# Setting constants on VectorE, evacuating a transpose in chunks, and moving two gate tiles in a fused attention and MLP block

## The chip, the cores and the metric

The kernel runs on one core of one Trainium2 chip. The time is the device time of one execution in microseconds (us). The core has five engines with a queue each: TensorE (PE, matrix products), VectorE (DVE), ScalarE (ACT), GpSimd (POOL) and SyncE (SP, which here only issues DMAs). Products land in PSUM, which has eight banks of 128 partitions by 2 KB; DVE and ACT read them from there.

## The reference

For 2048 tokens of width 448, a layer norm without scale or shift gives `xn`. Two branches start from it.

```
qkv  = xn @ wqkv                      # 16 heads of 28
phi(t) = where(t > 0, t + 1, exp(t)) + 1e-6
kv   = sum over tokens of phi(k) v    # per head, 28 x 28
z    = sum over tokens of phi(k)
s    = (phi(q) kv / (phi(q) z + 1e-6)) @ wo

h    = max(xn @ w1 + b1, 0) ** 2      # 1792 wide
g    = silu(h @ w2 + b2)
out  = x + s * g
```

Inputs and output are bfloat16.

## The kernel before, in words

Tokens come in 16 tiles of 128 (number `si`) or four groups of 512 (number `g`). The width of 448 is three chunks of 128 and one of 64. `xn` is stored 512 wide per token tile: its last 64 columns are copied once more behind column 448 (`dup`, L707, for tiles 0 to 3, and L490 for the others), so that the transposed tile has the 64-row chunk in both halves of the partitions and two 64-row products can run beside each other.

The kernel does not write instructions in a fixed order. Each helper adds operations to a `Program` with an engine, what they read and write, and an estimated duration. `schedule` (L88) then makes a list schedule. PE and SP keep the order in which their operations were added. ACT, DVE and POOL take, of the operations that are ready soonest, the one that is due first, where "due" is worked out backwards from PE's order. An operation with a rank (while `pr.hot` is set, L1097 to L1119) may run only in its written order among the ranked ones of its engine. `emit` (L235) adds semaphore waits. PSUM banks are given out by the schedule too: a new buffer takes the bank that comes free first.

The parts that matter here:

- **Constants.** POOL writes `ident` (identity for transposes), `kvm` (128 x 1792), `hmask`, `zmask`, `ehd` and `zsb` with memsets (L363 to L395, L853), and cuts masks out of `hmask` (2), `zmask` (8) and `ehd` (4) with affine selects. DVE writes only `wz` (zeros for dummy products) and `onesr` (L371, L372).
- **Start.** PE runs 50 dummy products (`warm`, L1064, L1095). Meanwhile x tiles 0 and 1 arrive in a DMA each, tiles 2 and 3 in one. Each tile takes statistics on DVE (`ln_stats`, L461 and L463), a reciprocal root on ACT (`ln_rstd`, L470 and L474), a normalisation on DVE (`ln_norm`, L481), and the `dup`.
- **First transposes.** `x_transpose0` (L713) transposes two token tiles on PE, chunk by chunk (L724), and copies the result out of PSUM to `xT`. For tiles 0 and 1 ACT copies chunks 0, 2 and 3 (L744), DVE chunk 1 (L750). For tiles 2 and 3 DVE makes two copies of two chunks each. All later tiles are transposed by DMA (L495).
- **First hidden products.** `pe_part` (L567) computes the first seven 128-row pieces of h for group 0 in two halves of 256 tokens (L695): part 0 from token tiles 0 and 1, part 1 from tiles 2 and 3.
- **The main run.** `quads` (L1073) takes units in fours: `K` (k of one token tile), `Q` (128 columns of q of a group), `H` (128 rows of h of a group). For K and Q, `phi` (L592) runs exp on ACT and two operations on DVE (L599, L606). For H, ACT adds the bias and takes the maximum (L666), and DVE or ACT squares (L680, L681). `qx` (L647) computes the last 64 columns of q. POOL sums phi(k) over tiles (`zsum`, L626).
- **Gate tiles.** `gg` (L954) computes one token tile of h @ w2 with 14 products, from all 14 squared pieces of its group; DVE adds b2 (L981). Tiles 0 to 3 are done early, between the quads.

The order of PE around the moved part is, in L1142 to L1146, quad H1.8 to H1.11, `qx(0)`, gate tiles 0 and 1, quad Q0.2 H1.12 Q1.0 H1.13. After it come the layer norm of tiles 12 to 15 and the quads of group 2.

Of the kernel before, what the change touches and what calls it, by code (L numbers as in the profile page):

```python
# [7 lines left out]
AF = mybir.ActivationFunctionType  # L8

P = 128  # L10
S, D, F = 2048, 448, 1792
# [33 lines left out]
class Program:  # L45
# [14 lines left out]
    def add(self, eng, emit, reads=(), writes=(), dur=0.2, alts=(), nbytes=0):  # L60
        reads = [p for r in reads for p in self.aliases.get(r, (r,))]
        op = Op(eng, emit, reads, writes, dur, alts, nbytes)
        op.lead = self.lead
        if self.hot is not None:
            self.hot += 0.01
            op.prio = op.rank = self.hot
        for t in op.reads:
            w = self.writer.get(t)
            if w is not None:
                op.raw.add(w)  # L70
            self.readers.setdefault(t, []).append(op)
        for t in op.writes:
            w = self.writer.get(t)
            if w is not None and w is not op:
                op.deps.add(w)
            for r in self.readers.get(t, ()):
                if r is not op:
                    op.deps.add(r)
            self.writer[t] = op
            self.readers[t] = [r for r in self.readers.get(t, ()) if r is op]  # L80
        op.raw.discard(op)
        op.deps |= op.raw
        for d in op.deps:
            d.succ.append(op)
        self.ops.append(op)
        return op
# [208 lines left out]
def bass_recurrent_scan__linear_attn_block__dense_activation_squared_relu__prompt_kernel(  # L295
    nc, A_x, A_wqkv, A_wo, B_x, B_w1, B_b1, B_w2, B_b2, out
):
    with ExitStack() as es:
# [47 lines left out]
        def pool(fn, writes, reads=(), dur=0.3):  # L346
            add("pool", fn, reads, writes, dur)
# [15 lines left out]
        pool(lambda e, _: e.memset(ident[:, :], 0.0), ["ident"])  # L363
        select(ident[:, :], "ident", [[-1, P]], 0, 1, 1.0, ALU.not_equal)
        pool(lambda e, _: e.memset(eps5[:, :], 1e-5), ["eps5"], dur=0.1)
        add("pool", lambda e, _: e.memset(kvm[:, :, :], 0.0), [], ["kvm"], 1.0).prio = -50.0

        def vset(ap, val, name, again=False, dur=0.08):
            add("dve", lambda e, _: e.memset(ap, val), [name] if again else [], [name], dur)

        vset(wz[:, :], 0.0, "wz")  # L371
        vset(onesr[:, :], 1.0, "onesr")  # L372
        pool(lambda e, _: e.memset(eps6[:, :], 1e-6), ["eps6"], dur=0.1)

        def late_constants():
            hv = hmask[:, :].rearrange("p (b j) -> p b j", b=HC)
            pool(lambda e, _: e.memset(hv, 1.0), ["hmask"])
            select(hv, "hmask", [[-DH, HC], [0, DH]], 0, 1, 0.0)
            select(hv, "hmask", [[DH, HC], [0, DH]], DH - 1, -1, 0.0)
            pool(lambda e, _: e.memset(zmask[:, :, :], 1.0), ["zmask"])  # L380
            for view, pat, base in (
                (zmask[:, 0:3, :], [[P, 3], [-DH, 32]], 0),
                (zmask[:, 3, :], [[-DH, 32]], 384),
                (zmask[:, 4, :], [[-DH, 32]], 320),
            ):
                select(view, "zmask", pat, base, 1, 0.0)
                select(view, "zmask", [[-a, n] for a, n in pat], DH - 1 - base, -1, 0.0)
            select(zmask[:, 3, :], "zmask", [[0, 32]], 63, -1, 0.0)
            select(zmask[:, 4, :], "zmask", [[0, 32]], -64, 1, 0.0)
            pool(lambda e, _: e.memset(ones[:, :], 1.0), ["ones"], dur=0.1)  # L390
            pool(lambda e, _: e.memset(ehd[:, :], 0.0), ["ehd"], dur=0.5)
            ev = ehd[:, :].rearrange("p (h j) -> p h j", h=NH)
            for g in range(NG):
                select(ev, "ehd", [[-1, NH], [0, DH]], -32 * g, 1, 1.0, ALU.not_equal, dur=0.6)
# [83 lines left out]
        def ln_norm(si):  # L478
            add(
                "dve",  # L480
                lambda e, _: e.tensor_scalar(  # L481
                    out=xn[:, si, 0:D], in0=x_tok[:, si, :], scalar1=mv[:, si, 0:1],
                    scalar2=rstd[:, si : si + 1], op0=ALU.subtract, op1=ALU.mult,
                ),
                [("x", si), ("mv", si), ("rstd", si)], [("xn", si)], 0.36,
            )
# [80 lines left out]
        def pe_part(us, part, cs=(0, 1, 2)):  # L567
            def f(e, _):
                last = None
                for k in cs:  # L570
                    for u in us:
                        last = u[2](e, slice(0, 128), k, k == 0, False, part)
                return last

            need = {("xTp", 2 * part, k) for k in cs} | {w for u in us for w in u[1]}
            banks = [u[0] for u in us]
            add(
                "pe", f, sorted(need, key=str) + (banks if part or cs[0] else []), banks,
                len(us) * len(cs) * MM(256) + 0.01,
            )  # L580
# [123 lines left out]
            reads = xnames(g) if full else []  # L704
            return b, reads + w1names(fi // 4), mm, lambda: h_out(b, g, fi), 512

        def dup(lo, hi):  # L707
            add(
                "dve", lambda e, _: e.tensor_copy(xn[:, lo:hi, D:512], xn[:, lo:hi, 384:D]),
                [("xn", k) for k in range(lo, hi)], [("xnd", k) for k in range(lo, hi)], 0.12,  # L710
            )

        def x_transpose0(lo, between=None):  # L713
            bs = [Buf("T"), Buf("T"), None, Buf("T")] if lo == 0 else [Buf("T")] * 4
            bs[2] = bs[0]

            def piece(cs, tail):
                def f(e, _):
                    last = None
                    for c in cs:  # L720
                        v = ps(bs[c])[:, :].bitcast(bf)
                        for k in (0, 1):
                            o = (c * 2 + k) * P
                            last = e.transpose(v[:, o : o + P], xn[:, lo + k, c * P : (c + 1) * P], ident[:, :])  # L724
                    return last

                add(
                    "pe", f, [(("xnd" if tail else "xn"), lo + k) for k in (0, 1)] + ["ident"],
                    list(dict.fromkeys(bs[c] for c in cs)), len(cs) * 0.114,
                )  # L730

            if lo == 0:
                piece((0, 1, 2), False)
                piece((3,), True)
            else:
                piece((0, 1, 2, 3), True)
            src = lambda c0, c1: (
                ps(bs[c0])[:, :].bitcast(bf)[:, c0 * 256 : c1 * 256].rearrange("p (c k t) -> p c k t", c=c1 - c0, k=2)
            )
            dst = lambda c0, c1: xT[:, lo : lo + 2, c0:c1, :].rearrange("p k c t -> p c k t")  # L740

            def on_act(c):
                return add(
                    "act", lambda e, _: e.activation(out=dst(c, c + 1), in_=src(c, c + 1), func=AF.Copy),  # L744
                    [bs[c]], [("xTp", lo, c)], 0.39,
                )

            def on_dve(c0, c1):
                return add(
                    "dve", lambda e, _: e.tensor_copy(dst(c0, c1), src(c0, c1)), [bs[c0]],  # L750
                    [("xTp", lo, c) for c in range(c0, c1)], 0.1 + 0.16 * (c1 - c0),
                )

            if lo == 0:
                on_act(0)
                on_dve(1, 2)
                on_act(2)
                between()
                return on_act(3)
            on_dve(0, 2)  # L760
            return on_dve(2, 4)

        def bias_columns():
# [86 lines left out]

                add("dve", zops, [b, "zmask", "zsb0"], [("zsb", v)], 0.2)

        pool(lambda e, _: e.memset(zsb[:, :, :], 0.0), ["zsb0"], dur=0.15)  # L853

        def fold_wo(c):
            b = Buf("M")
# [207 lines left out]
        def warm(n, cost=0.1, after=()):  # L1064
            def f(e, _):
                last = None
                for _i in range(n):
                    last = e.matmul(ps(wb)[:, 0:P], wz[:, :], wz[:, :], start=True, stop=True)
                return last

            add("pe", f, ["wz", *after], [wb], n * cost)
# [20 lines left out]
                x_transpose(si, si + step)  # L1092
            pr.lead = 0.0

        warm(50, 0.092)  # L1095
        H0 = {fi: hh(0, fi, fi >= 7) for fi in range(NF)}
        pr.hot = -100.0  # L1097
        ln_stats(0)
# [4 lines left out]
        ln_rstd(1, 2)  # L1103
        bias_columns()
        ln_norm(1)
        dup(1, 2)
        ln_stats(2)
        x_transpose0(0, lambda: ln_rstd(2, 3))
        ln_stats(3)
        ln_rstd(3, 4)  # L1110
        ln_norm(2)
        ln_norm(3)
        dup(2, 4)
        warm(6, 0.056)
        for c in range(3):
            pe_part([H0[i] for i in range(4)], 0, (c,))
# [1 line left out]
        t23 = x_transpose0(2)  # L1118
        pr.hot = None  # L1119
        pe_part([H0[6]], 0)  # L1120
        pe_part([H0[i] for i in range(4)], 1, (0, 1))
        pe_part([H0[i] for i in range(4)], 1, (2,))
        tails = lambda *u: pe_tails(*u, need=[("xTp", lo, 3) for lo in (0, 2)])
        tails(H0[0], H0[2])
        tails(H0[1], H0[3])
# [14 lines left out]
        for i in range(1, 8):  # L1140
            zsum(i)
        quads("H1.8 H1.9 H1.10 H1.11")  # L1142
        qx(0)
        gg(0)
        gg(1)
        quads("Q0.2 H1.12 Q1.0 H1.13")  # L1146
        ln(12, 16, lead=2)
        quads("K2.0 H2.0 K2.1 H2.2 K2.2 H2.1 K2.3 H2.3 H2.4 H2.5 H2.6 H2.7")
        for i in range(8, 12):
# [83 lines left out]
```

## Time and profile before

| | |
|---|---|
| median of 11 runs | 150.06 us (149.68 to 150.81) |
| the profiled execution's own time | 150.03 us |
| its span, first to last instruction | 148.3 us |
| mean granted TensorE clock | 0.998 |
| PE busy | 142.1 us (96%) |
| DVE busy | 97.5 us (66%) |
| ACT busy | 79.9 us (54%) |
| POOL busy | 36.8 us (25%) |

The 1.73 us between the span and the execution's time lie before its first and after its last recorded instruction. Times below are us from the start of the span. A busy time is the sum over the engine's instructions without overlap. DMAs and waits are not counted as busy. An instruction's row starts when it was sent to its engine, so an instruction that waits for the one before it or for a shared resource has a longer row. The page's cut of the span into 40 slices shows PE at nine tenths or more in all but the first three and the last. The chain that ended last is PE for 79% and DVE for 15%.

### The profile page before, as it was taken

How to read it: one execution, taken by the hardware profiler on the slowest of the kernel's cores; microseconds unless marked ns; L12 is line 12 of the kernel's file. 1: busy time of each engine (PE TensorE's matmuls, PEld its weight loads, DVE VectorE, ACT ScalarE, POOL GpSimd, SP SyncE). 2: the span in 40 equal slices, each digit the busy share in tenths (PEclk: the TensorE clock that was granted, in tenths of full speed). 3: DMA queues.
4: the chain of work that ended last, by engine and by line, in shares of the span. 5: the costliest groups of instructions: out<-in, count | busy, mean ns of one | idle time of the engine just before them, and what ended most of it. 6: DMA issues, size and time to landing. Idle time of an engine off the chain costs nothing.

```text
span 148.3 us, 2855 instructions
## 1 busy us (share of the span) xinstructions
PE 142.1 (96%) x1136; PEld 70.9 (48%) x1136; DVE 97.5 (66%) x215; ACT 79.9 (54%) x152; POOL 36.8 (25%) x55
## 2 busy tenths in 40 slices
PE   7889999999999999999999999999999999999990
PEld 7765444443444445444443554454444544545450
DVE  2879899999987896158999510069683517226343
ACT  3435897898886983188879721997411110310200
POOL 8850025253000353000650000000000908209100
PEclk9999999999999999999999999999999999999999
DMA  4998699910747000000000000000000111202112
GB/s 81 339 313 219 175 213 377 261 50 0 53 93 133 8 4 0 0 0 4 0 2 0 4 0 0 0 4 2 0 0 4 62 62 47 77 0 66 62 62 62
DMA packets 16025, 10.53 MB, mean 71 GB/s; under 512 B 7372, under 2 KB 15628, under 8 KB 16012
## 3 DMA queue, kind: packets, MB, share of 16 engines
q1 hardware_dynamic: 15824, 10.28, 26.4%
q8 instruction: 9, 0.15, 0.4%
q10 hardware_dynamic: 188, 0.07, 0.2%
q14 instruction: 4, 0.03, 0.1%
HBM read 6.94 MB, written 1.84 MB: 59 GB/s over the span
## 4 chain that ended last, share of the span: by engine, by line
PE 79%; DVE 15%; DMA 2%; ACT 1%; issue 0%; SPq 0%; DVEq 0%
PE pb L964 29%; PE pb L699 18%; PE pb L779 6%; PE pb L1018 6%; PE pb L616 5%; PE pb L640 5%; DVE r L680 3%; DVE xn L481 3%; DVE pk L606 2%; DMA x_tok<-in_A_x_dram 2%; PE pb L695 2%; DVE pk L599 1%; PE pb L1054 1%; DVE st L461 1%; PE pb L785 1%; PE pb L865 1%
## 5 line engine op out<-in xcount | busy, mean ns | idle before, releaser
L964 PE MATMUL pb<-w,r 128*128 128x448 bf16 x224 | 44.3, 353 | 0.6 <-DVE r L680 0.6
L666 ACT ACTIVATE r<-pb,b1f 128x512 bf16<-128x512 f32 x54 | 33.8, 690 | 10.0 <-PE pb L699 9.9
L699 PE MATMUL pb<-xT,w 64*128 64x512 bf16 (+1 forms) x291 | 38.5, 376 | 0.0
L964 PEld LDWEIGHTS pb<-w,r 128*128 128x128 bf16 x224 | 21.1, 98 | 21.8 <-issue 1.7
L626 POOL TENSOR_TENSOR zacc<-zacc,pk 128x448 f32<-128x448 f32 x13 | 14.4, 1106 | 40.7 <-DVE pk L606 40.2
L991 ACT ACTIVATE gbuf<-gbuf 128x448 bf16<-128x448 bf16 x15 | 8.5, 581 | 29.7 <-DVE gbuf L981 29.7
L1007 POOL TENSOR_TENSOR obuf<-obuf,x_tok 128x448 bf16<-128x448 bf16 x12 | 12.0, 1029 | 48.7 <-DVE obuf L1001 48.7
L699 PEld LDWEIGHTS pb<-xT,w 64*128 64x128 bf16 (+1 forms) x291 | 14.2, 94 | 16.6 <-issue 0.4
L981 DVE TENSOR_TENSOR gbuf<-pb,b2b 128x448 bf16<-128x448 f32 x15 | 9.3, 623 | 16.5 <-PE pb L964 16.4
L680 DVE TENSOR_TENSOR r<-r 128x512 bf16<-128x512 bf16 x34 | 18.0, 562 | 3.0 <-ACT r L666 3.0
L1001 DVE TENSOR_TENSOR obuf<-pb,gbuf 128x448 bf16<-128x448 f32 (+2 forms) x17 | 9.2, 592 | 7.2 <-PE pb L1018 4.7
L681 ACT ACTIVATE r<-r 128x512 bf16<-128x512 bf16 x22 | 13.3, 635 | 0.0
L616 PE MATMUL pb<-w_qkv,xT 64*128 64x448 bf16 x112 | 13.2, 349 | 0.0
L948 DVE TENSOR_TENSOR pqT<-pqT,pb 128x512 bf16<-128x512 bf16 x12 | 7.4, 681 | 8.6 <-PE pb L925 8.6
L461 DVE BATCH_NORM_STATS2 st<-x_tok 128x6 f32<-128x448 bf16 x16 | 9.3, 616 | 2.7 <-DMA x_tok<-in_A_x_dram 2.7
L640 PE MATMUL pb<-xT,w_qkv 64*128 64x512 bf16 x84 | 11.0, 376 | 0.0
L699 PE MATMUL pb<-xT,w_1r 64*128 64x512 bf16 x56 | 10.3, 377 | 0.0
L606 DVE SCALAR_TENSOR_TENSOR pk<-pb,pk 128x448 bf16<-128x448 f32 x16 | 9.7, 621 | 0.3
L594 ACT ACTIVATE pk<-pb 128x448 bf16<-128x448 f32 x16 | 7.8, 541 | 3.4 <-PE pb L616 3.4
L779 PE MATMUL pb<-pk,xn 128*128 128x448 bf16 x48 | 9.4, 353 | 0.0
L606 DVE SCALAR_TENSOR_TENSOR pqT<-pb,pqT 128x512 bf16<-128x512 f32 x12 | 8.3, 692 | 0.4
L616 PEld LDWEIGHTS pb<-w_qkv,xT 64*128 64x128 bf16 x112 | 5.5, 94 | 6.0
(89 smaller groups left out, 130.4 us busy)
## 6 DMA issues: line engine op xcount, KB each, us to landing
out_dram<-obuf SPq DMA_DIRECT2D x15, 112.0 KB, 1.7
w<-in_B_w_dram SPq DMA_DIRECT2D x1, 1568.0 KB, 9.3
x_tok<-in_A_x_dram SPq DMA_DIRECT2D x3, 448.0 KB, 4.4
w<-in_B_w_dram SPq DMA_DIRECT2D x3, 384.0 KB, 5.0
w_qkv<-in_A_wqkv_dram SPq DMA_DIRECT2D x3, 336.0 KB, 5.1
w_o<-in_A_wo_dram SPq DMA_DIRECT2D x1, 392.0 KB, 9.2
w_qkv<-in_A_wqkv_dram SPq DMA_DIRECT2D x6, 56.0 KB, 4.6
x_tok<-in_A_x_dram SPq DMA_DIRECT2D x2, 112.0 KB, 2.5
```

The costliest lines, as they stand in the source:

```text
L461: op = add("dve", lambda e, _: e.bn_stats(st6[:, si, :], x_tok[:, si, :]), [("x", si)], [("st", si)], 0.58)
L606: lambda e, _: e.scalar_tensor_tensor(out=slot, in0=ps(buf)[:, 0:n], scalar=1.0 + 1e-6, in1=slot, op0=ALU.add, op1=ALU.max),
L616: return e.matmul(ps(b)[:, 0:D], xT[rw, si, c, :], w_qkv[rw, c, D : 2 * D], start=start, stop=stop)
L626: lambda e, _: e.tensor_tensor(out=o[:, :], in0=pk[:, 0, :] if i == 1 else zacc[:, :], in1=pk[:, i, :], op=ALU.add),
L640: return e.matmul(ps(b)[:, 0:512], w_qkv[rw, c, m * P : (m + 1) * P], xT[rw, 4 * g : 4 * g + 4, c, :], start=start, stop=stop,)
L666: rl = lambda e, _: e.activation(out=slot, in_=ps(b)[:, 0:512], func=AF.Relu, bias=b1f[:, fi : fi + 1])
L680: return e.tensor_tensor(out=slot, in0=slot, in1=slot, op=ALU.mult)
L681: return e.activation(out=slot, in_=slot, func=AF.Square)
L699: return e.matmul(ps(b)[:, 0:512], lhs, xT[rw, 4 * g : 4 * g + 4, c, :], start=start, stop=stop, skip_group_check=not full,)
L779: last = e.matmul(ps(b)[:, 0:D], xn[:, si, c * P : (c + 1) * P], pk[:, si, :], start=(si == 0), stop=(si == NT - 1),)
L964: last = e.matmul(ps(b)[:, 0:D], r2[:, fi, si * P : (si + 1) * P], w_2[:, fi, :], start=(fi == 0 and part is None), stop=(fi == NF - 1),)
L1007: lambda e, _: e.tensor_tensor(out=ob, in0=ob, in1=x_tok[:, si, lo:hi], op=ALU.add),
```

## The change

Five memsets move from POOL to DVE, or to the beginning of DVE's program: `zsb`, `hmask`, `zmask`, `ehd` and `kvm`. The selects stay on POOL. The dummies are 43 instead of 50, with another estimate of their cost. The `dup` of tile 1 runs on ACT. That of tiles 2 and 3 becomes two, the first ahead of tile 3's normalisation. The evacuation of the second transposes is three copies (chunk 0, chunk 1, chunks 2 and 3) instead of two, and the products that read it are added chunk by chunk. `qx(0)` and gate tiles 0 and 1 come behind the quad Q0.2 H1.12 Q1.0 H1.13.

```diff
-        add("pool", lambda e, _: e.memset(kvm[:, :, :], 0.0), [], ["kvm"], 1.0).prio = -50.0
...
         vset(wz[:, :], 0.0, "wz")
         vset(onesr[:, :], 1.0, "onesr")
+        vset(zsb[:, :, :], 0.0, "zsb0")
+        vset(hmask[:, :], 1.0, "hmask", dur=0.15)
+        vset(zmask[:, :, :], 1.0, "zmask", dur=0.2)
+        vset(ehd[:, :], 0.0, "ehd", dur=0.3)
+        vset(kvm[:, :, :], 0.0, "kvm", dur=1.0)
...
-            pool(lambda e, _: e.memset(hv, 1.0), ["hmask"])
...
-            pool(lambda e, _: e.memset(zmask[:, :, :], 1.0), ["zmask"])
...
-            pool(lambda e, _: e.memset(ehd[:, :], 0.0), ["ehd"], dur=0.5)
...
-        def dup(lo, hi):
+        def dup(lo, hi, act=False):
+            if act:
+                add(
+                    "act",
+                    lambda e, _: e.activation(out=xn[:, lo:hi, D:512], in_=xn[:, lo:hi, 384:D], func=AF.Copy),
+                    [("xn", k) for k in range(lo, hi)], [("xnd", k) for k in range(lo, hi)], 0.2,
+                )
+                return
...
-            on_dve(0, 2)
+            on_dve(0, 1)
+            on_dve(1, 2)
             return on_dve(2, 4)
...
-        pool(lambda e, _: e.memset(zsb[:, :, :], 0.0), ["zsb0"], dur=0.15)
...
-        warm(50, 0.092)
+        warm(43, 0.106)
...
         ln_norm(1)
-        dup(1, 2)
+        dup(1, 2, True)
...
         ln_norm(2)
+        dup(2, 3)
         ln_norm(3)
-        dup(2, 4)
+        dup(3, 4)
...
-        pe_part([H0[i] for i in range(4)], 1, (0, 1))
-        pe_part([H0[i] for i in range(4)], 1, (2,))
+        for c in range(3):
+            pe_part([H0[i] for i in range(4)], 1, (c,))
...
         quads("H1.8 H1.9 H1.10 H1.11")
+        quads("Q0.2 H1.12 Q1.0 H1.13")
         qx(0)
         gg(0)
         gg(1)
-        quads("Q0.2 H1.12 Q1.0 H1.13")
```

## The prediction

> **What bounds the kernel.** I read the page first: TensorE (PE) is busy 142.1 of the 148.3 us span, VectorE (DVE) only 97.5. Nearly all of PE's work is fixed, so the question is where PE stands still. The list of PE's waits (us in total, times, longest us) gives all of it:
>
> ```profile
> PE pb L1068 <- DVE wz L369: 1.1, 1, 1.1
> PE pb L964 <- DVE r L680: 0.6, 1, 0.6
> PE pb L724 <- DVE xn L481: 0.5, 1, 0.5
> PE pb L724 <- DVE xn L709: 0.4, 1, 0.4
> PE pb L695 <- DVE xT L750: 0.2, 1, 0.2
> ```
>
> The first is the lead-in to the dummies and stays. Three belong to the first transposes, one (0.6) to gate tile 0. The chain that ended last (start, us, what) says which count:
>
> ```profile
> 1.26 2.98 DMA x_tok<-in_A_x_dram
> ...
> 9.47 0.26 DVE xn L709
> 9.73 0.05 issue
> 9.78 0.63 PE pb L724 x8
> 10.41 0.02 issue
> 10.44 0.44 DVE xT L750
> 10.87 0.05 issue
> 10.92 1.48 PE pb L695 x12
> ...
> 35.26 2.02 DVE r L680 x6
> 37.28 0.05 issue
> 37.33 5.47 PE pb L964 x28
> ```
>
> From 4.24, when the second x tile lands, until 10.92 the chain runs over DVE and ScalarE (ACT); then PE until 20.26, DVE until 37.28, PE to the end. So two points set the time: when PE starts at 10.92, and when the squares (L680) let gate tile 0 start at 37.33. The third view is the timeline up to 10.5 (start, us, engine, line, operation), first DVE's, then POOL's:
>
> ```profile
> 0.96 0.17 DVE L369 MEMSET onesr<- 1x128 bf16 x1
> 2.94 0.63 DVE L461 BATCH_NORM_STATS2 st<-x_tok 128x6 f32<-128x448 bf16 x1 [1.81 <-DMA x_tok<-in_A_x_dram]
> ...
> 5.42 0.49 DVE L709 COPY xn<-xn 128x64 bf16<-128x64 bf16 x1
> ...
> 6.13 0.59 DVE L709 COPY xn<-xn 128x64 bf16<-128x64 bf16 x1
> ...
> 8.97 0.47 DVE L481 TENSOR_SCALAR xn<-x_tok,mv,rstd 128x448 bf16<-128x448 bf16 x1 [0.32 <-ACT rstd L474]
> 9.47 0.25 DVE L709 COPY xn<-xn 128x128 bf16<-128x128 bf16 x1
> ```
> ```profile
> 5.41 0.47 POOL L391 MEMSET ehd<- 128x448 bf16 x1
> 6.02 3.16 POOL L357 TENSOR_SCALAR_AFFINE_SELECT ehd<-ehd 128x448 bf16<-128x448 bf16 x4
> ```
>
> The 64-column copies take 0.49 and 0.59, though the same copy of 128 columns (L490) takes 0.19 later, when POOL is idle. Each ends within 0.05 us of a POOL instruction: the ehd memset (5.88), and the first ehd select (6.02 + 0.67 = 6.69).
>
> **The memsets.** DVE gets zsb, hmask, zmask, ehd and kvm. From wz to onesr, 64 words took 0.07 us, one word a cycle of about 1 ns; wz is written as uint32, so the zero tiles cost half their columns: 80 + 224 + 896, and 112 + 160 fp32 words, 1472 words or 1.53 us. DVE's gap before the first statistics is 1.81 (1.13 to 2.94): they fit with some 0.2 to spare, and another 0.48 of idle time stands before the second statistics at 4.26, which alone are on the chain. Cost nothing; cover gone beyond some 0.7. [...] I take 1.53, since the wz row shows the packed form.
>
> **POOL.** It loses kvm (1.59), zmask, zsb, ehd and hmask memsets (0.24 + 0.23 + 0.47 + 0.19). ident comes first, the zmask selects start near 1.25 instead of 3.05. From the first zmask select to the first ehd select is now 2.97; without the zsb and ehd memsets and the gaps behind them (about 0.6) it is 2.35, so the ehd selects, 0.81 apart, start near 3.6, 4.4, 5.2, 6.0 and end near 6.8. They are not gone from the normalisation: they now stand under both norms and the first dup. [...] By the uncontended row (a copy at 0.19 or less) dup(0) loses its 0.3 and norm(1) is held by its rstd (5.66) until 6.0. [...]
>
> **dup of tile 1 to ACT.** It takes 0.20 to 0.25 there (L474's one column 0.20, L744's 256 columns 0.36), hidden under the six transposes before the tail that needs it (0.5). In ACT's queue it stands before L744's copies, which wait for those same transposes. On DVE 0.59 goes: the statistics of tile 2 run from 6.35 rather than 6.72. What is late next is ACT: its two L744 copies start near 6.95 instead of 6.70, rstd(2) (0.5) and the third copy (0.35) follow, so rstd(3) ends near 8.9, as now (8.93). So DVE's gain is caught there. Behind it norm(3) is free of POOL (0.33 rather than 0.47), dup(2) runs in DVE's 0.32 idle before norm(3), and dup(3) alone takes at most 0.19, likely 0.15, against 0.25. Second transposes near 9.49 instead of 9.78: **-0.29**. POOL's hmask selects are over by 7.6. PE's earlier block (18 products, 0.107 each, from about 7.4) ends by 9.4.
>
> **Chunk-wise evacuation.** The first product needs only chunk 0. A one-chunk copy took 0.26 (7.36), a two-chunk copy 0.44: **-0.17**. The second chunk lands 0.26 later, while four products (0.43) of the first run: one more instruction, hidden. H0[6] on PE fills the time meanwhile and ends about when the copy does. PE starts at 10.46, **-0.46** with both.
>
> **Fewer dummies.** The windows of the dummies (PE columns are busy us and count, edge-crossers counted twice):
>
> ```profile
> 3.50:4.00 0.50, 0.50 (x7) 0.50 (x6) 0.00 (x0) 1.00 0.65 211
> 4.00:4.50 0.50, 0.50 (x9) 0.50 (x7) 0.00 (x0) 1.00 1.01 319
> 4.50:5.00 0.50, 0.50 (x13) 0.50 (x11) 0.00 (x0) 1.00 0.99 329
> ```
>
> The rate doubles near 4.3. Seven fewer at 0.056 end 0.39 earlier, at 5.2, into idle time: nothing gained, nothing paid, if the fast rate stays.
>
> **The gate tiles moved.** Quad Q0.2 H1.12 Q1.0 H1.13 (3.03 us in the chain from 42.80) goes before qx(0), gate tiles 0 and 1. PE's own sum is the same; its data (weights, xT of tokens 0 to 7) are used earlier already. Its four PSUM banks are those of H1.4 to H1.7, which ACT has emptied by 34.4, before PE needs them at 35.1. Gate 0 on PE's path: 37.33 - 0.61 - 0.46 + 3.03 = 39.29. DVE must finish group 0's squares: 37.28, plus two phis moved ahead of them (2 x (0.28 + 0.69) = 1.94), less the part of the early start that DVE passes on. It is busy 16.70 of 17.00 us from 20 to 37, its statistics of tokens 8 to 11 wait for x until 16.93, so at most 0.3 passes: 38.9 to 39.2. PE and DVE meet; bounds for the wait left are 0 and 0.6 (all of it back), I take 0.1, near the balance. **-0.51.** K2 follows gate 1 at the same offset; its DMA transposes were issued at 37.41 and the first pair lands 3.7 later, against 44.7. They may be issued up to 2 us later without cost, and none of SP's loads stands behind them in need.
>
> **Sum.** -0.46 - 0.51 = -0.97. Span 148.3 to 147.33; the profiled run's own 150.03 has 1.73 around the span: 149.06; that run lies 0.03 under the median of 150.06. I say **149.1**.
>
> **Rivals.** (1) *No collision at the start*: POOL's selects fall between DVE's copies, norm(1) ends at 6.0, the chain gains another 0.35: 148.7. For it, the selects leave 0.14 gaps; against it, norms longer than these. (2) *DVE remains the bound at gate 0*: the moved phis, or norms beside POOL's sums (four took 2.82 at 32.44, 1.32 at 14.50), hold the squares; half to all the gain goes back: 149.55 to 150.05. (3) *PE goes back to half rate.* After 5.2 PE has one tiny transpose until 6.4, 1.2 idle rather than 0.46, then short bursts. [...] If it comes back for as long as the dummies needed to lift it (3.2 us from 1.05), the products of 7.4 to 10.6 cost half of that, 1.6: 150.7. [...]
>
> **How the numbers follow.** Forecast 0.52 (its own range 148.8 to 149.5), (1) 0.10, (2) 0.22, (3) 0.16. A measurement of this kernel tells about 0.2% (0.3 us) from no change. Forecast, (1) and half of (2) are faster: 0.73; the other half of (2) 0.11; (3) 0.16. The range 148.55 to 150.3 leaves out (3) and the tail of (1).
>
> **What would show it.** DVE's memsets end before 2.9; ehd selects lie at 3.6 to 6.8 and dup(0) still takes about 0.6; second transposes near 9.5, PE's unbroken run from about 10.5; the wait of L964 for L680 at 0.2 or less. Wrong if PE's matmul rate halves after 5.2, if gate 0 still waits 0.5 or more, or if a PSUM wait turns up at the moved quad.

## The result, and the profile after

The changed kernel takes 148.87 us (median of 13 runs, 148.75 to 149.8) against 150.07 for the kernel before. The ratio is 0.993, with a 95% interval of 0.9913 to 0.9946. The forecast was 149.1. In a second comparison on the chip the same kernel took 149.37 against 150.15 (0.9941, 0.9923 to 0.996). The experiments show the most likely reason why the two medians differ by half a microsecond.

The profiled execution took 148.77 us with a span of 147.0, 1.3 less than before. PE's waits, in the same form as before (us in total, times, longest us), are now these two:

```profile
PE pb L1076 <- DVE wz L368: 1.1, 1, 1.1
PE pb L732 <- DVE xn L482: 1.0, 1, 1.0
```

The lead-in to the dummies is as it was. The second wait is the end of the dummies until the first transposes, longer than before (0.5) because the dummies end earlier. The waits for the dup, for the evacuation and at gate tile 0 are all gone. The chain that ended last (start, us, what) shows the two points that the prediction named:

```profile
5.29 0.68 DVE xn L717
5.97 0.29 DVE xn L482
6.26 0.05 issue
6.31 0.62 PE pb L732 x8
6.93 0.34 PE pb L1076 x6
7.26 0.03 issue
7.29 2.14 PE pb L696 x18
9.43 0.52 PE pb L732 x8
9.95 0.02 issue
9.98 0.30 DVE xT L758
10.28 0.05 issue
10.33 1.48 PE pb L696 x12
...
38.05 1.10 PE pb L656 x8
39.15 5.40 PE pb L972 x28
```

PE's unbroken run starts at 10.33 instead of 10.92, 0.59 earlier. Gate tile 0 (L972) follows the product before it with no gap. Before, the chain came to it over VectorE, with a wait of 0.61. The two make 1.20 of the difference.

Between the first and the second transposes the chain now runs over PE alone: six more dummies and the 18 products on tiles 0 and 1, which end at 9.43. VectorE has its last dup done before that, at 9.26. In the kernel before it was VectorE's last dup (9.47 to 9.73) that let the second transposes start.

The timeline of VectorE, and behind it one row of POOL's, shows the start and the squares:

```profile
2.53 0.17 DVE L368 MEMSET onesr<- 1x128 bf16 x1
3.00 0.63 DVE L462 BATCH_NORM_STATS2 st<-x_tok 128x6 f32<-128x448 bf16 x1 [0.30 <-DMA x_tok<-in_A_x_dram]
...
4.49 0.77 DVE L482 TENSOR_SCALAR xn<-x_tok,mv,rstd 128x448 bf16<-128x448 bf16 x1
...
5.29 0.68 DVE L717 COPY xn<-xn 128x64 bf16<-128x64 bf16 x1
...
34.81 2.43 DVE L681 TENSOR_TENSOR r<-r 128x512 bf16<-128x512 bf16 x7
37.15 2.20 DVE L462 BATCH_NORM_STATS2 st<-x_tok 128x6 f32<-128x448 bf16 x4
39.27 0.28 DVE L600 TENSOR_SCALAR pqT<-pqT 128x512 bf16<-128x512 bf16 x1
```
```profile
3.64 3.13 POOL L357 TENSOR_SCALAR_AFFINE_SELECT ehd<-ehd 128x448 bf16<-128x448 bf16 x4
```

The memsets end at 2.70 and VectorE still waits 0.30 for x. The ehd selects run from 3.64 to 6.77, and under them the first normalisation takes 0.77 (0.36 before) and the first dup 0.68 (0.49). The last squares of group 0 end at 37.2, almost 2 us ahead of gate tile 0.

### The profile page after: what moved, and what is told of

Read it like the earlier page. It is cut to its first block, busy times and chain, and to the rows that moved or that the text cites. A ratio compares the mean times of both kernels' runs of the same rounds, so it can differ in the third digit from the quotient of the medians.

```text
span 147.0 us, 2842 instructions
## 1 busy us (share of the span) xinstructions
PE 141.5 (96%) x1129; PEld 70.6 (48%) x1129; DVE 96.6 (66%) x221; ACT 79.9 (54%) x153; POOL 34.2 (23%) x50
## 4 chain that ended last, share of the span: by engine, by line
PE 93%; DVE 3%; DMA 1%; issue 0%; DVEq 0%
PE pb L972 29%; PE pb L700 26%; PE pb L617 7%; PE pb L788 6%; PE pb L641 6%; PE pb L1026 6%; PE pb L696 3%; PE pb L1062 2%; PE pb L656 1%; DMA x_tok<-in_A_x_dram 1%; PE pb L794 1%; PE pb L873 1%; DVE st L462 1%; PE pb L732 1%; DVE xn L482 1%; PE pb L933 1%
## 5 line engine op out<-in xcount | busy, mean ns | idle before, releaser
L972 PE MATMUL pb<-w,r 128*128 128x448 bf16 x224 | 44.3, 353 | 0.0
L972 PEld LDWEIGHTS pb<-w,r 128*128 128x128 bf16 x224 | 21.1, 98 | 21.1 <-issue 2.4
L681 DVE TENSOR_TENSOR r<-r 128x512 bf16<-128x512 bf16 x34 | 16.2, 508 | 3.9 <-ACT r L667 3.9
```

What stands on the lines that cost most here:

```text
L681: return e.tensor_tensor(out=slot, in0=slot, in1=slot, op=ALU.mult)
L972: last = e.matmul(ps(b)[:, 0:D], r2[:, fi, si * P : (si + 1) * P], w_2[:, fi, :], start=(fi == 0 and part is None), stop=(fi == NF - 1),)
```

## The experiments

There were twelve runs, in three groups. Each is set against the kernel before on the same chip (150.23, 150.15 and 150.10 in the three groups). Line numbers are those of each kernel's own file, so the same line can stand some lines further down than in the kernel before.

### The gate tiles alone

```diff
         quads("H1.8 H1.9 H1.10 H1.11")
+        quads("Q0.2 H1.12 Q1.0 H1.13")
         qx(0)
         gg(0)
         gg(1)
-        quads("Q0.2 H1.12 Q1.0 H1.13")
```

> The kernel before with the quad Q0.2 H1.12 Q1.0 H1.13 moved ahead of qx(0) and gate tiles 0 and 1, nothing else. Theory (two separate bounds, the start of PE's unbroken run and gate tile 0): the run still starts near 10.9, the wait of gate tile 0 for L680 (0.6) is gone, so the time is 0.5 to 0.6 us lower. Rival (VectorE holds gate tile 0 also at its later place): a wait of 0.3 or more comes back at gate tile 0 or at the moved quad, and the gain is 0.3 or less.

It took 149.52, a ratio of 0.9961 (0.9945 to 0.9978), or 0.6 less (0.71 between the two medians). In its profile the run starts at 10.80, as it would before, and gate tile 0 waits for nothing. PE's waits do have one line that the first profile of the kernel before did not have:

```profile
PE pb L699 <- ACT r L666: 0.3, 1, 0.3
```

This line does not come from the move. The load of x tiles 4 to 7 landed late in this execution, at 12.40, and the second profile of the kernel before has the same line (more on this load below). So the move is worth its 0.6 alone. The rival is out: PE's waits have no line for gate tile 0, which starts at 39.98, behind the products of `qx(0)` (L655), which PE began at 38.88.

### The first 11 us alone

The reverse of the diff above, applied to the changed kernel.

> The changed kernel with gate tiles 0 and 1 back at their old place, so only the edits of the first 11 us. Theory: PE's unbroken run starts 0.5 to 0.6 earlier (near 10.35), but VectorE, full from 20 to 37 us, passes on only part of it; gate tile 0 waits 0.8 to 0.9 instead of 0.6, and the time is 0.3 to 0.4 lower. Rival (the two gains simply add): gate tile 0 waits 0.6 as before, and the time is 0.6 lower. Together with the gate move alone, the theory's two runs add up to less than the 1.2 of the whole change, the rival's to all of it.

It took 150.36, a ratio of 1.0009 (0.9994 to 1.0025): no gain at all. Both expectations missed. The profile, of one of its fastest executions (149.53), makes it stranger: the run starts at 10.39 and gate tile 0 waits 0.62, so there the start passes on 0.5. Most executions lost it somewhere that this profile does not show.

### The selects taken out of the way

```diff
-            for g in range(NG):
-                select(ev, "ehd", [[-1, NH], [0, DH]], -32 * g, 1, 1.0, ALU.not_equal, dur=0.6)
+        def ehd_selects():
+            ev = ehd[:, :].rearrange("p (h j) -> p h j", h=NH)
+            for g in range(NG):
+                pool(
+                    lambda e, _, g=g: e.affine_select(
+                        out=ev, in_=ev, pattern=[[-1, NH], [0, DH]], compare_op=ALU.not_equal, fill=1.0,
+                        base=-32 * g, channel_multiplier=1,
+                    ),
+                    ["ehd"], ["ehd", ("xnd", 3)], dur=0.6,
+                )
...
         pr.hot = None
+        ehd_selects()
```

> The changed kernel with the four ehd selects on POOL made to wait for the dup of token tile 3, so that they run behind the first transposes; the hmask selects come ahead of them, near 3.6. Theory (the selects shut VectorE's normalisations and copies out): the rows of the first normalisation and the first dup fall from 0.77 and 0.68 to about 0.36 and 0.2, the first transposes start 0.3 to 0.8 earlier than 6.31, and PE's unbroken run starts 0.3 to 0.7 earlier than 10.33, with the time as much lower. Rival (these rows are long for another reason, or ACT or the arrival of w1 or x bounds the start instead): rows unchanged, or rows short and PE's run at 10.2 to 10.4, the time within 0.1 of the changed kernel's.

It took 149.53 (148.5 to 150.23), where the changed kernel had 148.87 and 149.37 in other groups. Here is VectorE's timeline of the first normalisation and dup:

```profile
4.54 0.36 DVE L491 TENSOR_SCALAR xn<-x_tok,mv,rstd 128x448 bf16<-128x448 bf16 x1
4.94 0.18 DVE L726 COPY xn<-xn 128x64 bf16<-128x64 bf16 x1
```

The collision is gone. The rows fall to 0.36 and 0.18, the first transposes start at 5.88 and the run at 10.00. As to the rows the theory holds. The time, expected to be 0.3 to 0.7 lower, did not fall: PE waits 1.1 later on, and the chain that ended last, between 9 and 18 us, says for what:

```profile
6.57 5.90 DMA x_tok<-in_A_x_dram
12.48 0.02 issue
12.50 2.21 DVE st L471 x4
14.70 0.29 DVE mv L473 x4
14.99 0.02 issue
15.02 0.31 ACT vep L480
15.32 0.02 issue
15.35 0.20 ACT rstd L484
15.55 0.59 ACT r L676
16.14 0.05 issue
16.18 1.04 PE pb L709 x8
```

The load of x tiles 4 to 7, issued near 6.6, lands at 12.48. VectorE's statistics of these tiles wait for it, ACT's reciprocal roots wait for the statistics, and behind the roots in ACT's queue stand the operations (L676) that empty PSUM banks. PE gets no bank until 16.18. An earlier start runs into this all the same, so in such an execution it is worth nothing.

### The same two kernels once more

> The kernel before, unchanged, for a second profile of its first 11 us. In the first profile the statistics of token tile 1 wait for its x until 4.26, in that of the changed kernel they run at 3.76 already. [...] Rival (the change itself made the x tiles land earlier): it lands at 4.2 to 4.3 again, and every profile of a kernel with the changed start shows 3.8 or less.

The second profile of the kernel before (150.21) has the statistics of tile 1 at 3.72, not 4.26, and the second transposes at 9.50, so the first profile showed a late x tile 1. And it has this row of VectorE:

```profile
12.28 2.21 DVE L461 BATCH_NORM_STATS2 st<-x_tok 128x6 f32<-128x448 bf16 x4 [1.36 <-DMA x_tok<-in_A_x_dram]
```

In the first profile these statistics started at 11.41. The load was issued at 6.59 in both. PE's run starts 0.28 earlier than in the first profile (10.64), yet gate tile 0 starts 0.17 later (37.50), behind squares that end at 37.45. That is how the run with the first 11 us alone can have lost its gain: with x late, VectorE's chain to the squares follows x, not PE.

> The changed kernel, unchanged, beside the three that follow. The x tiles 4 to 7 landed at 10.7 in its first profile, and at 11.3 to 12.5 in those of the other kernels, which issue the same loads in the same order. Theory (this landing differs between executions, and where it is late VectorE's statistics of tiles 4 to 7, and on ACT the reciprocal roots that wait for them, hold back the first emptying of PSUM banks, so that PE waits at L700 near 15): executions spread from 148.75 to 149.9, with single values near 148.75 where x lands before about 11. Rival (the changed kernel itself makes x land early): executions stay within 0.1 of 148.75.

The changed kernel spread from 148.78 to 150.02 over 12 executions, four of them at or below 148.84. Over both groups it has 25 executions with a median of 149.16, 0.9 to 1.0 below the kernel before. The second profile (148.84) starts its run at 10.32 and the statistics of tiles 4 to 7 at 11.59, and PE does not wait: a landing up to there is covered. None of its slower executions was caught in a profile, so that they have a late landing is concluded from the next run.

### The load of x tiles 4 to 7 moved ahead of wk

```diff
-        load_k("sp", w_qkv, A_wqkv, "wk", D, 2 * D)
         load_x(4, 8)
+        load_k("sp", w_qkv, A_wqkv, "wk", D, 2 * D)
```

> The changed kernel with the load of x tiles 4 to 7 issued ahead of the three loads of wk instead of behind them, nothing else (1.8 us earlier on SP's queue). Theory (the late landing of x 4 to 7 is what spreads the times and costs the slower executions up to 1 us): VectorE waits for no x at the statistics of tile 4, PE does not wait for ACT at L700, and the median is 148.6 to 148.8, with most executions inside 0.2. Rival (the spread comes from elsewhere, or wk then lands too late for K0.0 at 14): the spread stays or the time is 0.3 or more above the changed kernel's.

148.85, and the five executions lie within 148.63 and 149.05. The slow part of the spread is gone. VectorE no longer waits for x at the statistics of tile 4, nor PE for ACT. This is what the theory said, with one point off: the median lies a little above the 148.6 to 148.8 expected. The profile is of the slowest of the five (149.05), and in it the run starts at 10.61 (see the last section, on PE's rate); whether the others lost time there is not shown. Three more kernels with the early x, below, have six executions each that lie within 0.13, 0.09 and 0.04. The one with the gate tiles at their old place spreads more.

> As the run before, and the ehd selects of POOL behind the dup of tile 3. Theory (in the run with late selects alone the start gained 0.33, from 10.33 to 10.00, and lost it again to the late x): now the gain is kept, the time is 0.3 to 0.4 below that of the changed kernel with early x, 148.3. Rival (another bound, such as the banks or the DVE chain behind, takes it): within 0.1 of it.

148.59 (148.46 to 148.69), a ratio of 0.9903 (0.9883 to 0.9922). The run starts at 10.02, and what the moved selects gain is kept in the main: 0.26 below the run before, a little less than expected. With four and five executions whose ranges touch, the size is not sharp. This is the fastest version; its median is 0.3 below the lower of the changed kernel's two.

> The edits of the first 11 us with early x, gate tiles 0 and 1 at their old place. Theory (with a late x VectorE's chain to the squares of group 0 starts at the landing, not at PE's start, so the start's gain was lost at gate tile 0 in the run without early x): gate tile 0 now waits about 0.6 and the time is 149.3 to 149.5, 0.6 above the same kernel with the gate tiles moved. Rival (VectorE, full from 20 to 37, holds gate tile 0 whatever x does): a wait of 0.9 or more, and 149.8 or above.

149.51, a ratio of 0.9968 (0.9956 to 0.998), with 14 of its 22 executions between 149.38 and 149.53. Gate tile 0 waits 0.6 as before, as the theory said. So the edits of the first 11 us are worth 0.5 (by the ratio) to 0.6 (between the medians) together with the early x, and nothing without it while the gate tiles stand at their old place. The kernel before with early x alone was not run, so how much of the 0.6 is the early x by itself stays open. The gate move adds 0.66 to this (149.51 to 148.85 in the same group). This is what the rival in the run of the first 11 us alone had said: the two gains add up, but only once x is in time.

### Single edits undone, all with the early x

One evacuation copy for chunks 0 and 1, as before the change:

```diff
-            on_dve(0, 1)
-            on_dve(1, 2)
+            on_dve(0, 2)
             return on_dve(2, 4)
...
-        for c in range(3):
-            pe_part([H0[i] for i in range(4)], 1, (c,))
+        pe_part([H0[i] for i in range(4)], 1, (0, 1))
+        pe_part([H0[i] for i in range(4)], 1, (2,))
```

> The changed kernel with early x, and the second evacuation as before the change: one copy of chunks 0 and 1, one of chunks 2 and 3, the products added for chunks 0 and 1 together. Theory (PE stands until the first copy ends): from the first of the second transposes to PE's unbroken run it is 1.14 again instead of 1.01, PE waits 0.15 to 0.2 for the copy, and the time is 0.13 to 0.17 above the 148.85 of the changed kernel with early x. Rival (H0[6] or something behind hides the copy): no wait, the time within 0.1.

148.94. The second transposes start at 9.34 and PE's run at 10.48, 1.14 later, with the wait from PE's timeline:

```profile
10.48 1.48 PE L696 MATMUL pb<-xT,w 128*128 128x256 bf16 x12 [0.19 <-DVE xT L758]
```

The split is worth this 0.13 to 0.19. The medians (148.94 and 148.85, from two groups) are too near each other to show it alone. The rival is out, as PE does wait.

The dup of tile 1 back on VectorE (`dup(1, 2)` in place of `dup(1, 2, True)`):

> The changed kernel with early x, the dup of tile 1 back on VectorE. Theory (this copy collides with a POOL select, 0.5 to 0.6 long, and pushes the statistics of tiles 2 and 3 back, which then set rstd(3) instead of ACT's own queue): statistics of tile 2 start 0.4 to 0.6 later than 6.17, the second transposes 0.2 to 0.4 later than 9.3 to 9.6, the time 149.05 to 149.25. Rival (ACT's queue alone sets rstd(3), as the prediction has it catch VectorE's gain): the second transposes and the time within 0.1.

149.19 (149.19 to 149.23). VectorE's timeline:

```profile
6.30 0.53 DVE L717 COPY xn<-xn 128x64 bf16<-128x64 bf16 x1
6.72 0.61 DVE L462 BATCH_NORM_STATS2 st<-x_tok 128x6 f32<-128x448 bf16 x1
```

The statistics of tile 2 move from 6.17 to 6.72 and the second transposes start at 9.75. VectorE has its last dup done at 9.69 here, so its chain alone allows no earlier start (PE's block of 18 products ends at 9.76). The edit is worth 0.3 between the medians (149.19 and 148.85, from two groups), more than any other that was undone. How much depends on PE: the second transposes stood at 9.32 in the changed kernel, but at 9.61 in the profile with early x, in which PE's rate rose late. The separate dups of tiles 2 and 3 and the seven fewer dummies were not undone by themselves.

The five memsets back on POOL, at their old places:

> The changed kernel with early x, the five memsets back on POOL at their old places. Theory (the selects lie between 6 and 9.3 then, and hit the normalisations of tiles 2 and 3 and their dups instead of norm(0) and dup(0)): first transposes at about 5.9 to 6.2 instead of 6.3, second ones 0.2 to 0.6 later than 9.3 to 9.6, the time 149.05 to 149.45. Rival (moving the memsets only moves the collision, with no net gain): the second transposes within 0.15, the time 148.7 to 149.0.

148.86 (148.8 to 148.93), so the memsets are worth nothing that can be measured. VectorE's timeline, and behind it a row of POOL's, shows why:

```profile
7.86 0.68 DVE L716 COPY xn<-xn 128x64 bf16<-128x64 bf16 x1
8.44 0.39 DVE L481 TENSOR_SCALAR xn<-x_tok,mv,rstd 128x448 bf16<-128x448 bf16 x1
8.86 0.52 DVE L716 COPY xn<-xn 128x64 bf16<-128x64 bf16 x1
```
```profile
6.22 3.13 POOL L357 TENSOR_SCALAR_AFFINE_SELECT ehd<-ehd 128x448 bf16<-128x448 bf16 x4
```

The first transposes start at 5.64 here, 0.67 earlier than with the memsets on VectorE, but now dup(2) and dup(3) run beside the selects and take 0.68 and 0.52 (0.18 each in the changed kernel), and the second transposes start at 9.44. Moving the memsets moved the collision from one pair of copies to the other. The rival was right.

Eight dummies in place of 43 (`warm(8, 0.57)`, which keeps the planned total):

> The changed kernel with early x and 8 dummies instead of 43, their planned cost unchanged so that every other queue keeps its order. Theory (the dummies are there to lift PE's rate, and half rate comes or stays where PE is idle): PE is idle from 2 to 5, its first products at 7.3 take 0.21 apiece instead of 0.107, that block ends near 11 instead of 9.4, and the time is 1.5 to 3 above 148.85. Rival (PE's rate is lifted by its own work in time, or the slow block is hidden under VectorE's chain): within 0.5 of 148.85.

151.14 (149.22 to 152.13 in 15 executions; 150.9 without the two longest). PE's timeline has the first 18 products at

```profile
7.79 4.05 PE L696 MATMUL pb<-xT,w 128*128 128x256 bf16 x18
```

where the changed kernel takes 2.14 for them. So half rate at this place costs about 2 us, and the dummies are needed. One execution took only 149.22; no profile shows whether PE's rate rose in time in it. In the profiles with 43 these products took 2.14 to 2.26.

## Why the prediction was right

- **The two bounds.** The sum had 0.46 from the start and 0.51 from gate tile 0. The first profiles of the two kernels have 0.59 and 0.61. The gate move gives 0.6 alone and 0.66 on top of the start; the start gives 0.5 to 0.6 with the early x and nothing by itself without it. So the bounds were the right ones, but the start's size depends on x. Against the second profile of the kernel before, whose run starts at 10.64, it is 0.31 and not 0.59.
- **The number.** That 149.1 came so near is luck in part. Of the 25 executions of the changed kernel 12 took 148.75 to 148.93, and 13 took 149.16 to 150.02. The forecast lies in the gap between, above the executions in which both gains are kept. And 148.87 is nearer to the first rival's 148.7 than to 149.1: the rows of VectorE speak against that rival, not the time.
- **Memsets.** "Cost nothing" is shown: they end at 2.70, before x tile 0. That they gain nothing either is shown by the run with the memsets on POOL. The sum gave them no term of their own, but its -0.29 has what they bring: norm(3) and dup(3) free of POOL (0.14 and 0.10 gained), against ACT's copies (L744) 0.25 later. The 1472 words took 1.58 us, from 0.98 to 2.56, against 1.53 in the sum, and kvm was written as 896 uint32 words, as the sum took it.
- **The selects beside VectorE.** The sum starts the statistics of tile 2 at 6.35 and ACT's copies (L744) at 6.95, both behind a norm(1) that ends 0.25 later than before, beside the ehd selects. No run shows this 0.25. What the profile of the changed kernel shows in its place: norm(0) ends at 5.26, dup(0) at 5.97 and norm(1) at 6.26, 0.16 later than before (6.10), the statistics of tile 2 start at 6.17 and ACT's copies (L752 there) at 6.85. With x tile 1 in time, norm(0) was sent at 4.49, just behind the start of the second select (4.45), and its row took 0.77 instead of 0.36; the dup behind it took 0.68. In the run of the first 11 us alone with early x, x tile 1 came late, and norm(0) kept its 0.36 while the dup behind it was long:

```profile
4.92 0.36 DVE L482 TENSOR_SCALAR xn<-x_tok,mv,rstd 128x448 bf16<-128x448 bf16 x1
5.32 0.66 DVE L717 COPY xn<-xn 128x64 bf16<-128x64 bf16 x1
```

norm(0) ends at 5.28, against 5.26. So the selects set these times, whether x tile 1 is early or late. The selects were predicted at 3.6 to 6.8 and ran at 3.64 to 6.77. With the selects away the rows fell to 0.36 and 0.18. The rival of a start without collision (another 0.35) did not come, but its price was about right when the selects were moved away: 0.33 in the start, 0.26 in the time.
- **The dup on ACT.** Statistics of tile 2 at 6.17 (said 6.35), second transposes at 9.32 (said 9.49). The time is near, the path is not: the sum had ACT's rstd(3) at 8.9 and VectorE's dup behind it, and took PE's block of 18 products as done just before, by 9.4. ACT ended rstd(3) at 8.61 and VectorE the dup at 9.26, and it was PE's block, to 9.43, that came last. By this chain, a further gain in VectorE's work on tiles 2 and 3 would have brought nothing. The term "-0.29" came out at -0.46 between the first two profiles, but at -0.18 against the second profile of before (9.50), in which x tile 1 is in time as in the changed kernel.
- **Chunk-wise evacuation.** Said 0.17, measured 0.13 in the start and a wait of 0.19 without it.
- **Fewer dummies.** "Nothing gained, nothing paid" holds for the profile that the sum was made on. It is not general. In the run with the gate tiles alone the rate rose late, the 50 dummies ended at 6.1, and the first transposes stood behind them at 6.17, though norm(1) was done at 5.52. There fewer dummies would let them start earlier. The half-rate rival did not come: PE paused for 1.0 us behind the 43 dummies, and the 18 products still took 2.14. Whether a longer pause would bring half rate back, and how long it would have to be, no run shows.
- **Gate tile 0.** The step "two phis moved ahead of" the squares was wrong. The list schedule put the squares ahead of the phis (34.81 to 37.2, then 39.27), so there were nearly 2 us in hand, and the wait left was 0, not 0.1. "At most 0.3 passes" was too little with x in time: in the profile of the first 11 us alone PE's run starts 0.53 earlier and gate tile 0 0.51 earlier.
- **What was missing.** The step "at most 0.3 passes" also named the wrong load, x tiles 8 to 11 at 16.93. It is x tiles 4 to 7 that can cap the start, landing between 10.7 and 12.5. The profile of before had a line for it (0.2 of waiting at 11.41), and the sum did not ask what it would be in another execution. With this load early the slow executions were gone, so it is most likely also the difference between 148.87 and 149.37.

## What to carry to other kernels

An edit that frees an engine early pays only as far as the next thing that engine needs is there; look at the loads just behind the edit, take a second profile of the same kernel, and ask how far each landing moves. Before moving work off POOL to spare VectorE, see where POOL's remaining instructions will lie: moving them under other copies of VectorE gained nothing here (148.86 against 148.85), moving them behind the critical stretch did (148.59 against 148.85). Where two paths end within 0.2 us of each other, as VectorE's dup and PE's block do here (9.26 and 9.43), read in the new chain which one came last. Two bounds in a row (start and gate tile) are tested apart and together, since one of them can look worthless alone.

## What the runs showed of the hardware that was not expected

- **Landing times.** The same load (448 KB, issued at 6.6 behind the same loads) took 4.1, 4.7, 4.8, 5.0, 5.7, 5.8 and 5.9 us to land in seven profiles. Issued near 4.8, ahead of 448 KB of wk, it took 4.4 to 5.8.
- **The moment when PE's rate doubles.** Before that moment a dummy costs 0.107 us (8 took 1.04 us, 43 took 4.77), after it 0.056 (six in 0.34). It lay near 4.3 in the first profiles and near 5.4 and 5.5 in two others (50 dummies took 4.53, 5.00 and 5.08 us). The 43 dummies took 3.94 us where it came earliest, near 4.0, and 4.77 where all of them were slow. The windows of the dummies (busy us and count) in the gate-tile run and in the changed kernel:

```profile
4.50:5.00 0.50, 0.50 (x8) 0.50 (x6) 0.00 (x0) 1.00 0.94 290
```
```profile
4.50:5.00 0.50, 0.50 (x12) 0.48 (x9) 0.00 (x0) 1.00 0.96 309
```

The granted clock reads 1.00 in both. Over the profiles the moment goes from 4.0 to beyond 5.5, where the last slow dummy of the 43 starts; what sets it is not shown. In the run of the changed kernel with early x the rate was still low at 6.31: its first eight transposes took 0.91 us instead of 0.62, and PE's block behind them and the run (10.61 rather than 10.33) came as much later.
